# The backward pass of a gated S4 block: h reloaded, parameter sums shared with GpSimd, gradient stores grouped, w2 padded in DRAM

## The chip, the cores and the metric

One core of a Trainium2 chip. The metric is the device time of one launch in microseconds, the median of the runs shown.

## The reference, cut to what matters

The kernel computes the forward pass and all gradients (a vjp) of

```python
xn  = layernorm(x)                                  # x: 2048 x 576
s   = fftconv(xn, K) + xn * Dskip                   # K[d,l] = Re sum_n C[d,n] exp(dtA[d,n] l) dtB[d,n], n = 0..127
h   = silu(xn @ w1) * (xn @ w3)                     # w1, w3: 576 x 4608
out = x + s * silu(h @ w2)                          # w2: 4608 x 576
```

with respect to x, A, B, C (each 576 x 128, real and imaginary), log_dt, Dskip, w1, w3 and w2. Data is bfloat16. out_0 is the output, out_1 the gradient of x, out_2 to out_9 those of the state space parameters, out_10, out_11, out_12 those of w1, w3, w2.

## The kernel before, in words

Rows are positions, in 16 tiles of 128. The forward builds the convolution kernel K, keeps its factors in DRAM (Q_dram, PZ_dram), computes gate and up for all positions and keeps them in DRAM (GI_dram), and h too (H_dram, read by the forward's own w2 product at L774 through DMA transposes named hc). The convolution is done with DFT matrices: spectra of xn (UH_dram) and of K (KH_dram), products of spectra on VectorE (cmul_acc, L594), inverse transforms on TensorE (idft_tile, L573).

The backward (L1066) interleaves four strands of work:

- *The feed-forward loop*, 18 groups of 256 hidden columns. phase6_load (L1125) loads gate and up for a group (gg_n, h_n), makes silu (gu_n) and its derivative on ScalarE in place, and multiplies on VectorE: L1153 makes derivative times up, L1154 makes h again as silu times up, in place. It also loads two row tiles of w2 into one of four padded SBUF rows (L1139, GpSimd's queue) and transposes them by DMA (w2T). phase6_group (L1157) multiplies by w2 (L1172), scales (L1178), and stores the two gradients of the hidden layer (GU_dram, GG_dram). phase6_grad2 (L1188) makes the gradient of w2, phase6_grad13 (L1206) those of w1 and w3; each result is copied from PSUM by ScalarE into a buffer gw or gw2 and stored through GpSimd's queue (L1205, L1222, L1231).
- *The convolution's backward* (conv_bwd_quarter, L866), four quarters of the channels. a3 holds a spectrum in three planes, the third a copy made on VectorE (spectrum_variants, L588). It multiplies the gradient by xn on VectorE (L893) for the gradient of Dskip, forms spectra products, transforms them back, and ScalarE writes each 128 x 144 result into gk_st by four instructions with strided outputs (L926, L927). A second set of products yields the gradient of xn (gx, started at L941, finished at L947, stored at L948).
- *The parameter sums* (param_quarter, L950), 36 chunks of 16 channels. Q is loaded by DMA transpose (qT), TensorE multiplies it with gK (L970) into two PSUM tiles T, VectorE multiplies these with PZ into pr_q (L977, four times per half chunk) and reduces each pr_q of 1024 numbers to 16 (L979, twice per half chunk). phase5_final (L982) comes after all chunks: it turns the sums S_all into the parameter gradients, for five blocks of up to 128 channels, and reloads the parameters for it.
- *The input gradient* (phase6_inputs, L1234), after the loop, 16 tiles: GG and GU come back through DMA transposes (ggc, guc), are multiplied by the transposed w1 and w3 (px, L1262), summed with gx from GXN_dram (L1265) and taken back through the layernorm (ln_bwd_tile, L1270). The transposed weights are in two parts: the first FA = 12 of 36 chunks are loaded early (wTA), the rest when the loop's buffers are free (wTB; the profile shows both under the name wTB_w).

What sets the order: each engine and each DMA queue runs its instructions in order. `self.at(us)` (L83) gives what follows a priority, in us, and the program's instructions are put in order by it as their inputs allow. The last call gives the numbers: backward(560, 36, 90, 15, 18, ...) puts groups 36 apart from 560, quarters of the convolution 90 apart, chunks 15 apart after the four quarters (from 920), and input tiles 18 apart after the loop (from 1208). Buffers come from pools with a number of buffers each; a tile waits until the one `bufs` before it is done. Pools of one side lie one upon the other, so a new pool waits for what lay there before. SyncE's queue (SP) carries all DMA transposes (nat_transpose, L1122) and most loads and stores.

Of the kernel before, what the change touches and what calls it, by code (L numbers as in the profile page):

```python
# [11 lines left out]
ALU = mybir.AluOpType  # L12
# [48 lines left out]
class K:  # L61
# [246 lines left out]
    def compute_W(self, pool, c, dsz):  # L308
        nc, cfg = self.nc, self.cfg
        N = cfg.N  # L310
        v = slice(0, dsz)
        Wr = pool.tile([P, N], FP32, name="Wr_c")
        Wi = pool.tile([P, N], FP32, name="Wi_c")
        t2 = pool.tile([P, N], FP32, name="Wt2")
        dtc = self.dt_col[v, c:c + 1]
        nc.vector.tensor_tensor(out=Wr[v], in0=self.C_re[v, c, :], in1=self.B_re[v, c, :], op=ALU.mult)
        nc.vector.tensor_tensor(out=t2[v], in0=self.C_im[v, c, :], in1=self.B_im[v, c, :], op=ALU.mult)
        nc.vector.tensor_tensor(out=Wr[v], in0=Wr[v], in1=t2[v], op=ALU.subtract)
        nc.vector.tensor_scalar(out=Wr[v], in0=Wr[v], scalar1=dtc, scalar2=None, op0=ALU.mult)
        nc.vector.tensor_tensor(out=Wi[v], in0=self.C_re[v, c, :], in1=self.B_im[v, c, :], op=ALU.mult)  # L320
        nc.vector.tensor_tensor(out=t2[v], in0=self.C_im[v, c, :], in1=self.B_re[v, c, :], op=ALU.mult)
        nc.vector.tensor_tensor(out=Wi[v], in0=Wi[v], in1=t2[v], op=ALU.add)
        nc.vector.tensor_scalar(out=Wi[v], in0=Wi[v], scalar1=dtc, scalar2=None, op0=ALU.mult)
        return Wr, Wi

# [262 lines left out]
    def spectrum_variants(self, A2, Az):  # L588
        nc = self.nc
        nc.vector.tensor_copy(out=A2[:, :, 1], in_=A2[:, :, 0])  # L590
        nc.vector.tensor_copy(out=A2[0:1, :, 1, 0, :], in_=Az[0:1, :, 0, :])
        nc.vector.memset(Az[0:1, :, 0, :], 0.0)

# [85 lines left out]
    def ffn_scratch(self):  # L679
        cfg = self.cfg  # L680
        D, DT, L, LT, FT = cfg.D, cfg.DT, cfg.L, cfg.LT, cfg.FT
        F = cfg.F
        self.FG = 256
        self.GI_dram = self.dram.tile([F // self.FG, P, 2, LT, self.FG], BF16, name="GI_dram")
        self.H_dram = self.dram.tile([LT, P, F], BF16, name="H_dram")
        self.GS_dram = self.dram.tile([4, P, LT, D // 4], BF16, name="GS_dram")
# [44 lines left out]
    def forward_tail(self, T0, TB, TQ, gctx):  # L731
# [19 lines left out]
        with pool(name="g_all", bufs=1, side="right") as gp, pool(name="o_ep", bufs=3, side="right") as ep, \  # L751
# [9 lines left out]
            with pool(name="o_ep1", bufs=1) as ep1, pool(name="o_h", bufs=2) as hp, \  # L761
# [4 lines left out]
                for n, t_ in enumerate(w2g):  # L766
                    nc.gpsimd.dma_start(out=t_[:], in_=aps["B_w2"][n * GRP * P:(n + 1) * GRP * P, :].rearrange(
                        "(c p) d -> p c d", p=P))
                for i0 in range(0, LT, 2):
# [69 lines left out]
    def ssm_bwd_conv(self, T0, TQ, ps):  # L839
# [3 lines left out]
        with self.tc.tile_pool(name="b_k", bufs=1, side="right") as kp, self.tc.tile_pool(name="b_z", bufs=2, side="right") as zp:  # L843
# [7 lines left out]
            for g in range(4):  # L851
                self.conv_bwd_quarter(g, kp, zp, ps, T0 + g * TQ, TQ)

    def ssm_bwd_params(self, T0, TC, S_all, ps):
        cfg = self.cfg
        D, LT = cfg.D, cfg.LT
        with self.tc.tile_pool(name="g_k", bufs=1, side="right") as gkp, self.tc.tile_pool(name="g_q", bufs=2, side="right") as qp:
# [5 lines left out]
            for g in range(4):  # L863
                self.param_quarter(g, gz, S_all, qp, ps, T0 + TC * g * D // 64, TC)

    def conv_bwd_quarter(self, g, kp, zp, ps, T0, TQ):  # L866
# [10 lines left out]
        for b in range(NB):  # L877
            a3 = kp.tile([P, 3, KT, W], BF16, name=f"a3_{b}")
            nc.sync.dma_start(out=a3[:, 1], in_=self.UH_dram[g, b, :, 0])
            nc.sync.dma_start(out=a3[:, 0], in_=self.UH_dram[g, b, :, 1])  # L880
            A2[b], Az[b] = a3[:, None, 1:3], a3[:, None, 0]
            self.spectrum_variants(A2[b], Az[b])
# [6 lines left out]
        for b in range(NB):  # L889
            prod = zp.tile([P, KT, W], BF16, name="gsxn")  # L890
            for tt in range(KT):
                t = b * KT + tt
                nc.vector.tensor_tensor(out=prod[:, tt, :].rearrange("p (h d) -> p h d", h=2),  # L893
# [12 lines left out]
        for i in range(NB - 1, -1, -1):  # L906
            self.at(T0 + TQ * (0.2 + 0.1 * (NB - 1 - i)))
# [12 lines left out]
            for oc in range(KT):  # L920
                t = i * KT + oc
                pt = ps.tile([P, 512], FP32, name="et_ps")
                self.idft_tile(pt, ZZ, oc)
                for h in range(2):
                    pv = pt[:, h * W // 2:(h + 1) * W // 2].rearrange("p (c d) -> p c d", d=8)
                    nc.scalar.activation(out=st[:, :, 0, :, h, t], in_=pv, func=ACT.Copy, scale=1.0 / 512)  # L926
                    nc.scalar.activation(out=st[:, :, 1, :, h, t], in_=pv, func=ACT.Copy, scale=self.lcol[:, t:t + 1])  # L927
# [7 lines left out]
        for j in range(NB):  # L935
            self.at(T0 + TQ * (0.6 + 0.1 * j))
# [3 lines left out]
            gx = zp.tile([P, KT, W], FP32, name="gx")  # L940
            nc.vector.tensor_tensor(out=gx[:], in0=gs[:, j * KT:(j + 1) * KT, :],  # L941
                                    in1=self.dskip_row[:, None, cs].to_broadcast([P, KT, W]), op=ALU.mult)
            for oc in range(KT):
                t = j * KT + oc
                pt = ps.tile([P, 512], FP32, name="et_ps")
                self.idft_tile(pt, Z, oc)
                nc.vector.tensor_tensor(out=gx[:, oc, :], in0=pt[:, 0:W], in1=gx[:, oc, :], op=ALU.add)  # L947
            nc.scalar.dma_start(out=self.GXN_dram[:, j * KT:(j + 1) * KT, cs], in_=gx[:])  # L948

    def param_quarter(self, g, gz, S_all, qp, ps, T0, TC):  # L950
# [3 lines left out]
        for cc in range(NQ):  # L954
# [6 lines left out]
            qT = qp.tile([P, 16, N], BF16, name="qT")  # L961
# [426 lines left out]
```

## Time and profile before

| | |
|---|---|
| median of 2 runs | 2041.88 us (2040.19 to 2043.56) |
| the profiled execution, its own time | 2058.91 us |
| its span, first to last instruction | 2057.1 us |
| mean granted TensorE clock | 0.947 |
| PE busy | 1772.9 us (86%) |
| DVE busy | 1428.3 us (69%) |
| ACT busy | 992.8 us (48%) |
| POOL busy | 366.5 us (18%) |
| DMA moved | 416.06 MB, mean 202 GB/s |

PE is TensorE's matmuls, PEld its weight loads, DVE VectorE, ACT ScalarE, POOL GpSimd, SP SyncE; a q behind the name is the engine's queue or sequencer. In a row of the timeline stand the start, the duration, the engine, the line of the kernel, and what is written from what. In a row of waits stand who waited for whom, and then us in total, times, and the longest. A row of stages has the stretch, its length, each engine's busy time with the number of instructions, the TensorE clock granted, the busy share of the DMA engines (above 1 means several packets in flight on one) and GB/s.

### The profile page before, as it was taken

How to read it: one execution, taken by the hardware profiler on the slowest of the kernel's cores; microseconds unless marked ns; L12 is line 12 of the kernel's file. 1: busy time of each engine (PE TensorE's matmuls, PEld its weight loads, DVE VectorE, ACT ScalarE, POOL GpSimd, SP SyncE). 2: the span in 40 equal slices, each digit the busy share in tenths (PEclk: the TensorE clock that was granted, in tenths of full speed). 3: DMA queues.
4: the chain of work that ended last, by engine and by line, in shares of the span. 5: the costliest groups of instructions: out<-in, count | busy, mean ns of one | idle time of the engine just before them, and what ended most of it. 6: DMA issues, size and time to landing. Idle time of an engine off the chain costs nothing. (4 is left out here: it accounts for less than half of the span.)

```text
span 2057.1 us, 42197 instructions
## 1 busy us (share of the span) xinstructions
PE 1772.9 (86%) x17174; PEld 1300.8 (63%) x17174; DVE 1428.3 (69%) x2772; ACT 992.8 (48%) x1668; POOL 366.5 (18%) x540
## 2 busy tenths in 40 slices
PE   2889999999699995999898998898899939989992
PEld 1534444444488874778777777786678727767771
DVE  7548888888287723686874868676789635858667
ACT  2778888888445544765646556343355200000000
POOL 4003333333312102111111211222111200000000
PEclk9999999999799997999999999999899969999996
DMA  3678888896957568465563655798898599999970
GB/s 83 204 290 301 306 298 302 290 320 248 283 140 175 136 139 260 125 179 168 165 179 96 195 155 164 196 264 205 183 208 203 163 232 216 198 216 226 208 150 22
DMA packets 595505, 416.06 MB, mean 202 GB/s; under 512 B 404912, under 2 KB 537136, under 8 KB 590704
## 3 DMA queue, kind: packets, MB, share of 16 engines
q1 hardware_dynamic: 539632, 264.00, 53.6%
q0 software_dynamic: 30544, 120.94, 17.2%
q10 hardware_dynamic: 25136, 28.44, 5.5%
q8 instruction: 134, 2.20, 0.4%
q14 instruction: 59, 0.48, 0.1%
HBM read 133.01 MB, written 188.01 MB: 156 GB/s over the span
## 5 line engine op out<-in xcount | busy, mean ns | idle before, releaser
L719 PE MATMUL pgu<-wmB_w,xnT 128*128 128x512 bf16 x1152 | 284.1, 382 | 1.1 <-ACT E_k L392 1.1
L1262 PE MATMUL px<-wTB_w,guc 128*128 128x288 bf16 x1152 | 243.7, 292 | 36.4 <-DMA guc<-GU_dram 24.1
L1262 PE MATMUL px<-wTB_w,ggc 128*128 128x288 bf16 x1152 | 245.3, 292 | 15.0 <-DMA wTB_w<-in_B_w_dram 9.1
L1218 PEld LDWEIGHTS <-xn_bf 128*128 128x128 bf16 x2304 | 226.2, 98 | 48.7 <-issue 20.7
L977 DVE TENSOR_TENSOR pr_q<-et_ps,pz 128x512 f32<-128x512 f32 x288 | 186.6, 680 | 96.2 <-PE et_ps L970 96.0
L1172 PE MATMUL ph<-w2T,goT 128*128 128x256 bf16 x1440 | 192.3, 286 | 8.8 <-ACT gh L1175 6.5
L719 PEld LDWEIGHTS <-xnT 128*128 128x128 bf16 x1152 | 103.5, 98 | 125.2 <-issue 20.9
L1279 ACT ACTIVATE t<-gx 128x576 f32<-128x576 f32 x16 | 10.9, 683 | 346.0 <-DVE gx L1265 311.3
L979 DVE TENSOR_REDUCE S_all<-pr_q 128x16 f32<-128x1024 f32 x144 | 173.9, 1211 | 0.4
L1200 PE MATMUL pgw<-go_o,h_n 128*128 128x288 bf16 x1152 | 160.9, 294 | 8.7 <-DVE h_n L1154 8.7
L1172 PEld LDWEIGHTS <-goT 128*128 128x128 bf16 x1440 | 144.1, 103 | 33.8 <-issue 7.8
L1262 PEld LDWEIGHTS <-guc 128*128 128x128 bf16 x1152 | 114.1, 100 | 68.9 <-DMA guc<-GU_dram 26.1
L1221 ACT CAST gw<-pgw 128x256 bf16<-128x256 f32 x144 | 53.7, 378 | 212.5 <-PE pgw L1218 169.7
L784 PE MATMUL po<-w2g,hc 128*128 128x288 bf16 x1152 | 148.9, 286 | 2.6 <-DMA hc<-H_dram 2.6
L1218 PE MATMUL pgw<-gg_n,xn_bf 128*128 128x256 bf16 x1152 | 132.5, 276 | 14.2 <-ACT gw L1221 14.2
L1262 PEld LDWEIGHTS <-ggc 128*128 128x128 bf16 x1152 | 113.8, 100 | 45.4 <-issue 9.6
L1200 PEld LDWEIGHTS <-h_n 128*128 128x128 bf16 x1152 | 113.9, 100 | 39.0 <-DVE h_n L1154 9.2
L1218 PE MATMUL pgw<-gu_n,xn_bf 128*128 128x256 bf16 x1152 | 132.3, 272 | 3.4 <-ACT gw L1221 2.0
L784 PEld LDWEIGHTS <-hc 128*128 128x128 bf16 x1152 | 111.5, 98 | 30.2 <-DMA hc<-H_dram 3.1
L722 ACT ACTIVATE s_t<-pgu 128x512 bf16<-128x512 f32 x144 | 87.4, 609 | 55.2 <-PE pgu L721 54.7
L1222 POOL DMA_DIRECT2D out_dram<-gw x144 | 77.7, 541 | 187.1 <-ACT gw L1221 184.0
L1175 ACT CAST gh<-ph 128x512 bf16<-128x512 f32 x144 | 83.7, 613 | 50.8 <-PE ph L1172 35.9
(305 smaller groups left out, 3726.1 us busy)
## 6 DMA issues: line engine op xcount, KB each, us to landing
GI_dram<-gu_t POOLq DMA_DIRECT2D x72, 512.0 KB, 5.7
H_dram<-h_t SPq DMA_DIRECT2D x72, 256.0 KB, 5.2
Q_dram<-q_k SPq DMA_DIRECT2D x36, 512.0 KB, 5.3
gg_n<-GI_dram POOLq DMA_DIRECT2D x18, 1024.0 KB, 5.7
h_n<-GI_dram POOLq DMA_DIRECT2D x18, 1024.0 KB, 8.7
GU_dram<-gu_n SPq DMA_DIRECT2D x36, 512.0 KB, 4.2
GG_dram<-gg_n SPq DMA_DIRECT2D x36, 512.0 KB, 7.5
E_dram<-E_k SPq DMA_DIRECT2D x18, 768.0 KB, 3.6
```

What stands on the lines that cost most here:

```text
L719: nc.tensor.matmul(pgu[:, j], lhsT=xnT[:, c, ts], rhs=wm[w][:, c, :], start=(c == 0), stop=False)
L722: nc.scalar.activation(out=s_t[:, :, q, :], in_=pgu[:, 0].rearrange("p (g f) -> p g f", g=ng), func=ACT.Silu)
L784: nc.tensor.matmul(pos[k][:, pi_, 0:pw], lhsT=hcs[k][:, fi, :], rhs=w2[fi][:, po:po + pw], start=(fi == 0), stop=(fi == FT - 1))
L977: nc.vector.tensor_tensor(out=pr[:, r], in0=T[r][:], in1=pz[:, s + r, h * 8:h * 8 + 8, :][:, :, None, :] .to_broadcast([P, 8, 2, AV]), op= ...
L979: nc.vector.tensor_reduce(out=S_all[:, 2 * s:2 * s + 2, d0:d0 + 8].rearrange("p k d -> p d k"), in_=pr[:].rearrange("p r d k a -> p d k r ...
L1172: nc.tensor.matmul(ph[j][:, k, :].rearrange("p (a f) -> p a f", f=P), lhsT=lw, rhs=rh, start=(n == 0), stop=(n == nfull))
L1175: nc.scalar.copy(out=gh[:, j], in_=ph[j][:])
L1200: nc.tensor.matmul(pgw[pi_][:, 0:pw], lhsT=hn[:, tt, fl * P:(fl + 1) * P], rhs=go_o[:, tt, po:po + pw], start=(tt == 0), stop=(tt == LT - 1))
L1218: nc.tensor.matmul(pw_[:, 0:FG], lhsT=self.xn_bf[:, tt, c * P:(c + 1) * P], rhs=nat[:, tt, :], start=(tt == 0), stop=(tt == LT - 1))
L1221: nc.scalar.copy(out=gw[:], in_=pw_[:, 0:FG])
L1222: nc.gpsimd.dma_start(out=aps[oname][c * P:(c + 1) * P, fb:fb + FG], in_=gw[:])
L1262: nc.tensor.matmul(px[pi_][:, 0:pw], lhsT=act[:, fi, :], rhs=wT[part][ai][:, f, po:po + pw], start=(fi == 0 and ai == 0), stop=(fi == FT - ...
```

## The change

- w2 is written to DRAM in the forward, padded from 576 to 640 columns (W2P_dram), from the tiles that the forward's w2 product uses; the backward transposes it from there. The four padded rows in SBUF go.
- L1154 goes. After L1153 h is loaded again from H_dram into the buffer of up.
- Convolution backward: the third plane of a3 is loaded, the corrections of one row go to GpSimd, and so do the products at L893 and the start of gx. Two inverse transforms share a PSUM bank; ScalarE copies them densely into a new buffer and GpSimd spreads them into gk_st. gx is stored in the natural order of the channels by two DMAs on SyncE's queue. New priorities spread the products evenly.
- Parameter sums: in each half chunk the first pr_q is folded by an addition on GpSimd, and VectorE reduces 512 numbers instead of 1024. qT has three buffers, pr_q a pool of its own; pz is loaded by SyncE's queue instead of ScalarE's. The final stage becomes final_block, called per block as soon as its chunks are there; its DMAs are on GpSimd's queue.
- Gradient stores go to ScalarE's queue; the four column tiles of w1's and w3's gradients are stored by one DMA.
- FA becomes 9. The priorities of the backward become backward(560, 40, 96, 15, 18, ...). In the input gradient the sum is made in place.

```diff
@@ forward_tail
+                wz = ep1.tile([P, 1, DT * P - D], BF16, name="wz")
+                nc.gpsimd.memset(wz[:], 0.0)
+                w2p = self.W2P_dram.rearrange("(c p) d -> p c d", p=P)
+                self.at(T0 + 150)
+                nc.sync.dma_start(out=w2p[:, :, D:DT * P], in_=wz[:].to_broadcast([P, FT, DT * P - D]))
+                for n, t_ in enumerate(w2g):
+                    nc.sync.dma_start(out=w2p[:, n * GRP:(n + 1) * GRP, 0:D], in_=t_[:])
@@ conv_bwd_quarter
-            nc.sync.dma_start(out=a3[:, 1], in_=self.UH_dram[g, b, :, 0])
-            nc.sync.dma_start(out=a3[:, 0], in_=self.UH_dram[g, b, :, 1])
+            for j, r in ((0, 1), (1, 0), (2, 0)):
+                nc.sync.dma_start(out=a3[:, j], in_=self.UH_dram[g, b, :, r])
...
-            self.spectrum_variants(A2[b], Az[b])
+            nc.gpsimd.tensor_copy(out=a3[0:1, 2, 0, :], in_=a3[0:1, 0, 0, :])
+            nc.gpsimd.memset(a3[0:1, 0, 0, :], 0.0)
...
-                nc.vector.tensor_tensor(out=prod[:, tt, :].rearrange("p (h d) -> p h d", h=2),
+                nc.gpsimd.tensor_tensor(out=prod[:, tt, :].rearrange("p (h d) -> p h d", h=2),
...
-            for oc in range(KT):
-                t = i * KT + oc
+            self.at(t0 + TQ * (0.0425 * (NB - i) + 0.06))
+            sd = sp.tile([P, KT, 2, W], BF16, name="gk_sd")
+            for o2 in range(0, KT, 2):
+                t = i * KT + o2
                 pt = ps.tile([P, 512], FP32, name="et_ps")
-                self.idft_tile(pt, ZZ, oc)
+                for j in range(2):
+                    self.idft_tile(pt[:, j * W:(j + 1) * W], ZZ, o2 + j)
+                nc.scalar.activation(out=sd[:, o2:o2 + 2, 0, :], in_=pt[:, 0:2 * W].rearrange("p (t d) -> p t d", t=2),
+                                     func=ACT.Copy, scale=1.0 / 512)
+                for j in range(2):
+                    nc.scalar.activation(out=sd[:, o2 + j, 1, :], in_=pt[:, j * W:(j + 1) * W], func=ACT.Copy,
+                                         scale=self.lcol[:, t + j:t + j + 1])
+            for k in range(2):
                 for h in range(2):
-                    pv = pt[:, h * W // 2:(h + 1) * W // 2].rearrange("p (c d) -> p c d", d=8)
-                    nc.scalar.activation(out=st[:, :, 0, :, h, t], in_=pv, func=ACT.Copy, scale=1.0 / 512)
-                    nc.scalar.activation(out=st[:, :, 1, :, h, t], in_=pv, func=ACT.Copy, scale=self.lcol[:, t:t + 1])
+                    nc.gpsimd.tensor_copy(out=st[:, :, k, :, h, i * KT:(i + 1) * KT],
+                                          in_=sd[:, :, k, h * W // 2:(h + 1) * W // 2].rearrange(
+                                              "p t (c d) -> p c d t", d=8))
@@ param_quarter
+                prs = []
                 for s in range(2):
-                    pr = qp.tile([P, 2, 8, 2, AV], FP32, name="pr_q")
+                    pr = rp.tile([P, 2, 8, 2, AV], FP32, name="pr_q")
...
-                    nc.vector.tensor_reduce(out=S_all[:, 2 * s:2 * s + 2, d0:d0 + 8].rearrange("p k d -> p d k"),
-                                            in_=pr[:].rearrange("p r d k a -> p d k r a"), op=ALU.add, axis=AX.XY)
+                    prs.append(pr)
+                nc.gpsimd.tensor_tensor(out=prs[0][:, 0], in0=prs[0][:, 0], in1=prs[0][:, 1], op=ALU.add)
+                out = lambda s: S_all[:, 2 * s:2 * s + 2, d0:d0 + 8].rearrange("p k d -> p d k")
+                nc.vector.tensor_reduce(out=out(1), in_=prs[1][:].rearrange("p r d k a -> p d k r a"), op=ALU.add, axis=AX.XY)
+                nc.vector.tensor_reduce(out=out(0), in_=prs[0][:, 0], op=ALU.add, axis=AX.X)
+            self.at(T0 + TC * (cc + 2))
+            ready(ch)
@@ backward
-        FA = 12
+        FA = 9
...
-            gwp = ffn.enter_context(pool(name="e_gw", bufs=4))
-            rowp = ffn.enter_context(pool(name="e_w2r", bufs=1))
+            gwp = ffn.enter_context(pool(name="e_gw", bufs=2))
...
-            self.ssm_bwd_params(T1, TC, S_all, ps)
-            self.at(T1 + TC * D // 16)
-            self.phase5_final(out, fix, S_all, ps)
+            self.ssm_bwd_params(T1, TC, fix, S_all, ps)
@@ phase6_load
-            w2r = self.w2rows[fi % len(self.w2rows)]
-            nc.gpsimd.dma_start(out=w2r[:, 0:D], in_=aps["B_w2"][fi * P:(fi + 1) * P, :])
-            self.nat_transpose(w2T[:, fl], w2r[:])
+            self.nat_transpose(w2T[:, fl], self.W2P_dram[fi * P:(fi + 1) * P, :])
...
-            nc.vector.tensor_tensor(out=hn[:, sl, :], in0=gu[:, sl, :], in1=hn[:, sl, :], op=ALU.mult)
+        nc.gpsimd.dma_start(out=hn[:], in_=self.H_dram[:, :, gi * FG:(gi + 1) * FG].rearrange("t p f -> p t f"))
@@ phase6_grad13
+            gw = gwp.tile([P, nfull, FG], BF16, name="gw13")
...
-                gw = gwp.tile([P, FG], BF16, name="gw13")
-                nc.scalar.copy(out=gw[:], in_=pw_[:, 0:FG])
-                nc.gpsimd.dma_start(out=aps[oname][c * P:(c + 1) * P, fb:fb + FG], in_=gw[:])
+                nc.scalar.copy(out=gw[:, c, :], in_=pw_[:, 0:FG])
+            nc.scalar.dma_start(out=aps[oname][0:nfull * P, fb:fb + FG].rearrange("(c p) f -> p c f", p=P), in_=gw[:])
```

## The prediction

> **What bounds the kernel now.** I read the page first: TensorE is busy 86% of a span of 2057.1 us, no other engine over 69%. So TensorE's work, 1773 us, is a floor that the change leaves (it removes no matmul), and only the 284 us in which TensorE stands idle can be won. The next view says where: busy time of each engine by stage. The boundaries are the first backward group, the first sum chunk of the parameter gradients, the last dense-gradient matmul, the end of the gap after it, and the last input-gradient matmul.
>
> ```profile
> core 0: us, PE busy (x) PEld busy (x) DVE busy (x) ACT busy (x) POOL busy (x), PEclk, DMA share, GB/s
> 560.00:795.00 235.00, 215.05 (x2173) 179.52 (x2172) 149.44 (x301) 110.53 (x192) 41.73 (x87) 0.96 0.62 154
> 795.00:1317.00 522.00, 464.54 (x4658) 395.67 (x4656) 370.70 (x769) 315.89 (x714) 92.11 (x170) 0.95 0.56 168
> 1317.00:1641.30 324.30, 291.66 (x3005) 245.38 (x3004) 238.32 (x336) 141.06 (x235) 66.54 (x117) 0.96 0.89 205
> 1641.30:1712.00 70.70, 27.46 (x242) 19.65 (x241) 28.25 (x40) 1.15 (x3) 1.07 (x2) 0.71 1.11 225
> 1712.00:2017.50 305.50, 290.05 (x2666) 229.83 (x2666) 212.58 (x412) 13.20 (x32) 0.00 (x0) 0.97 1.07 195
> 2017.50:2057.10 39.60, 0.22 (x2) 0.00 (x0) 26.66 (x141) 1.35 (x3) 0.00 (x0) 0.56 0.09 20
> ```
>
> Length minus PE busy gives TensorE's idle time: 20, 57, 33, 43, 15 and 39 us; the other 76 lie before 560 us, in code that the diff leaves alone. Third, the waits of TensorE (and one of ScalarE) in the two loop stages: us in total, times, longest.
>
> ```profile
> PE et_ps L582 <- ACT gk_st L927: 20.7, 22, 3.2
> PE et_ps L582 <- DVE gx L947: 9.8, 4, 3.6
> PE pgw L1200 <- DVE h_n L1154: 8.7, 1, 8.7
> ...
> PE et_ps L970 <- DMA qT<-Q_dram: 14.7, 4, 8.9
> PE pgw L1218 <- ACT gw L1221: 10.6, 3, 5.0
> ...
> ACT gw L1221 <- DMA out_dram<-gw: 23.4, 6, 7.1
> ```
>
> The first three are of the convolution stage: TensorE waits for PSUM banks that ScalarE empties in thin strided slices. The others are of the parameter stage: late transposes, and a staging buffer whose store has not landed. Fourth, the gap, in SyncE's timeline, and the tail, in VectorE's (start, us).
>
> ```profile
> 1659.32 33.77 SPq L1123 DMA_TRANSPOSE wTB_w<-in_B_w_dram  x10
> ...
> 2039.58 0.44 DVE L1265 TENSOR_TENSOR gx<-px,gxs 128x288 f32<-128x288 f32 x1
> 2039.94 0.27 DVE L1045 TENSOR_TENSOR ft<-ST,C_re_bf 64x128 f32<-64x128 f32 x1
> 2040.14 0.27 DVE L1048 TENSOR_SCALAR gout<-gr,dt_col 64x128 bf16<-64x128 f32 x1
> 2043.55 0.82 DVE L1291 SCALAR_TENSOR_TENSOR o<-t,rstd,go 128x576 bf16<-128x576 f32 x1
> ```
>
> TensorE is done at 2017.5, but the last tile's layernorm begins at 2039.6: it stands in VectorE's queue behind the small instructions of the final parameter block. That block, not the input gradient, sets the end.
>
> **What the Trainium skill says.** "SBUF — State Buffer", Who interferes with whom: a VectorE instruction with two SBUF inputs and a GpSimd instruction that reads SBUF lock each other out whole. The trace fits and doesn't prove it: the small GpSimd copy of L642 takes 346 ns in the median, 1130 at most. "GPSIMD Engine Reference", 3.1 Elementwise: two-input work costs about 2.6 cycles an element, about twice VectorE; the trace agrees (L247, 640 f32: 1.53 us). "TensorE: Matmul & The Clock Gate", Part 1: idle windows halve TensorE's clock; the trace agrees, with PEclk 0.71 in the gap against 0.95 to 0.97 in the dense stages. So an idle us saved brings somewhat more than itself. "DMA: Bandwidth & Descriptors", Issuing engines are not separate DMA queues: moving stores from GpSimd's queue to ScalarE's saves issue time, not bandwidth; nothing here shows it alone.
>
> **The change part by part**, against the profiled execution (2058.9 us, of which 1.8 lie outside the span).
>
> *Tail.* phase5_final is split into blocks that start when their chunks are summed. By the priorities, the last chunk moves from 36 us ahead of the last input tile to about 69 (chunks end at 944+36x15=1484, tiles at 1280+18x16=1568; before 1460 and 1496), and only two blocks are left by then: about 2 x 48 instructions x 0.25 us = 24 us of VectorE, in a stage where it is free 30% of the time. The last layernorm then runs from 2017.6 to 2022.4 (its own 4.8 us) and its store lands 5.2 us later (median of that issue): tail 10.5 instead of 39.6 us, **-29**. If the 12.7 us from the last store's issue to the end belong to that store, -21.
>
> *Convolution stage (522 us).* ScalarE's 256 strided copies (gk_st, 84 us of union) become 32 of 288 and 64 of 144 elements, about 32x0.40+64x0.25=29 us; GpSimd does the strided scatter, 64 copies of 288 elements. The trace has no such copy: by its 0.35 us for 144 elements on one partition 0.6 us, by the two-input rate 0.9; I take 0.8, 51 us. Nothing waits for it but the gK stores, a quarter ahead of their readers. Two transforms share a bank, so banks are freed sooner: the 20.7 goes, and half of the 9.8. VectorE loses the variant copies (9), gsxn (10), gx's start (12) and L1154 (72 x 0.66=48 over the loop): about 61 of its 371 us in this stage. On GpSimd the products cost 64x0.4=26 and gx's starts 16x1.6=26 us; if every GpSimd read locks VectorE out, its load returns to some 420 of 522, still under TensorE's 465. The extra a3 load (16 x 144 KB) is hidden by a DMA share of 0.56. Sum: -20.7-5-4 (gh copies behind the strided ones)-6 (gw waits)=**-36**.
>
> *h reloaded.* Not a product any more: a 1 MB load in 512 B pieces on GpSimd's queue, after L1153. I estimate 12 us to landing (512 KB stores with the same pieces: 4.2 and 7.5 us), less about 2 us of products that fall away. In before, L1154 ends 6 to 33 us ahead of the group's first L1200 (6.1, 10.8, 11.4 in the tightest), so ten us later costs some 4 us in one group and the first group's start: **+8**. Both ends: 0, if VectorE's relief brings L1153 forward; +46, if the load takes 20 us (the sum of what each group then lacks).
>
> *Parameter stage (324 us).* Per chunk VectorE did 8 x 0.65 + 4 x 1.21 = 10.0 us; two of the four reductions halve to about 0.65: 8.9. GpSimd's addition of 512 f32 is about 1.26 us by L247, and has two products and a full reduction (2.5 us) to hide behind; later than that by over 1.1 us, VectorE stalls one for one, and after three banks TensorE (L970). The PSUM tiles are freed 1.2 us earlier. Kernel gradients are staged by four, with one store instead of four, on ScalarE's queue: the waits for landed stores (23.4 and the 10.6 behind it) go; ScalarE gets 6 issues a group at about 0.4 us, hidden since it is busy 141 of 324. A third qT buffer and pz off ScalarE take half of the 14.7. About 22.4 chunks run before the input tiles instead of 17.8: 4.6 x 1.4 us of TensorE comes in. Less cold clock in both loop stages: -8 (estimate, from PEclk 0.95). Sum: -10.6-7+6.4-8=**-19**. The spread of the h loads over a DMA share of 0.89 is in the +8 and its upper end.
>
> *Gap.* FA 12 to 9 makes wTB 27 chunks instead of 24: 33.8 x 27/24, +4.2. By the pools' sizes the ggc tiles then lie over e_in only, not over the gw buffers, so the first transpose need not wait for the store that landed at 1648.6: up to -7, or -3 behind the qT already queued. **0**, from -10 to +8.
>
> *Input gradient.* 1.6 chunks fewer, in-place sum, pz no longer blocking ScalarE's loads: **-4** of the 15 us idle and the chunks' own time; final blocks in VectorE's 93 free us could cost as much.
>
> *Forward.* w2 padded: 10 writes on SyncE's queue past the hc transposes, 4608 pieces of 128 B among them, about 10 us of transfers under a DMA share of 0.62; hc loads now cost TensorE 2.6 us: **+4**, 0 to 10. GpSimd loses 36 w2r loads and their 122 us of waits. Memsets, pools and smaller buffers elsewhere: nothing on the chain.
>
> Sum: -29-36+8-19+0-4+4 = -76; I take **-73**, since a chain relieved shows the next wait. 2058.9-73=1986 for a profiled execution. The median of the runs shown, 2041.88, is 17.0 below the profiled one; the same difference gives **1969 us**.
>
> **Rivals.**
> - *Only the tail is won* (0.2). The h load takes 20 us in a DMA share near 0.9: loop stages -36-19+46=-9, with -29-4+4: -38, 2004; if GpSimd's new copies also cost TensorE 15 through locked-out VectorE, -23: 2019. For: 0.89 and 1.07 DMA share from 1317 us on. Against: eight groups had over 18 us to spare.
> - *The loop closes up* (0.12). with VectorE and ScalarE spread out TensorE reaches 97% here (from 300 to 350 us of the forward it is busy 49.67 of 50): of the loop's 90 idle us 65 go, 15 of cold clock, 11 in the gap, with the tail's 29: -120, 1922. Against: each relieved wait has another close behind.
> - *Slower* (0.08): GpSimd's queue holds up the loop. The h load waits in it for L1153, behind the eight activations (group 3: 911.1 to 922.7, 11.6 us); scatters, additions and products queued behind wait too, VectorE's reductions for them, and TensorE for banks. Two thirds of 11.6 us in 18 groups is 139: 2042-73+139=2108. It is slower than now from 4.1 us of lost TensorE per group, by 2% from 6.3. Against: GpSimd is busy 67 of 324 us, and additions can be queued ahead of the load.
>
> **How the numbers follow.** The forecast has 0.6; its own range is 1940 to 2000. The whole range, 1925 to 2025, leaves out the slower rival (0.08), part of the first rival (0.06) and part of the second (0.05). About 2% is what a measurement can tell from no change: under 2001 lie nearly all of the forecast (0.57), the second rival (0.12) and part of the first (0.06): 0.75; slower 0.07; within 2% 0.18.
>
> **What would show it.** Tail about 10 us, with the last layernorm right behind the last px. In the convolution stage no TensorE wait for gk_st, and PE busy near 93%. L1200 waiting for a DMA of h in one or two groups, not ten. TENSOR_REDUCE of half size near 0.65 us, not starting late behind GpSimd. A wTB row of about 38 us. I am wrong if h_n's DMA or a GpSimd addition leads the waits of TensorE or VectorE, or if the tail is still set by a parameter block.

## The result and the profile after

Measured: 2176.24 us (2171.02 and 2181.46) against 2041.88, a ratio of 1.0658 (95% interval 1.0542 to 1.0774): slower, where 1969 was forecast. The profiled execution took 2171.02 us, its span is 2169.2. (Medians and ratios of the runs further down leave out executions more than 1.5% above the fastest of the same kernel.) Busy time by stage of the changed kernel, with the boundaries of before (first backward group, first sum chunk, last dense-gradient matmul, end of the gap, last input-gradient matmul):

```profile
core 0: us, PE busy (x) PEld busy (x) DVE busy (x) ACT busy (x) POOL busy (x), PEclk, DMA share, GB/s
802.00:1380.00 578.00, 482.70 (x4737) 408.50 (x4736) 361.02 (x578) 277.47 (x570) 209.10 (x218) 0.91 0.61 174
1380.00:1730.50 350.50, 296.83 (x3026) 246.06 (x3027) 231.41 (x382) 131.66 (x224) 75.95 (x78) 0.92 0.93 216
1730.50:1796.50 66.00, 27.39 (x257) 19.98 (x256) 25.75 (x37) 0.37 (x1) 7.59 (x6) 0.66 1.07 219
1796.50:2162.10 365.60, 293.79 (x2573) 229.33 (x2569) 199.24 (x460) 13.65 (x34) 59.46 (x72) 0.91 1.00 159
2162.10:2169.20 7.10, 0.04 (x1) 0.00 (x0) 3.86 (x8) 0.78 (x2) 0.00 (x0) 0.87 0.06 21
```

The spans of the two profiled executions differ by 112.1 us, less than the medians' 134, because the profiled execution of before was 17 us above its median and that of the changed kernel 5 below. With each stage's exact ends in both traces the 112.1 us are: forward +7.9, convolution stage +43.0, parameter stage +38.3, gap +0.6, input gradient +54.6, tail -32.3. TensorE runs the same 17174 matmuls; their busy time grew by 24 us, at a granted clock of 0.91 and 0.92 instead of 0.95 to 0.97 in the three long stages, in which it now stands idle for 95, 54 and 72 us. What it waits for in the loop (us, times, longest):

```profile
PE ph L1176 <- ACT gh L1179: 41.5, 12, 14.0
PE pgw L1223 <- DVE gu_n L1182: 19.5, 6, 12.1
PE pgw L1204 <- DMA h_n<-H_dram: 13.2, 2, 9.2
PE pgw L1223 <- ACT gw L1225: 12.2, 3, 7.8
PE et_ps L564 <- DVE ZZ L922: 11.7, 4, 7.1
PE ph L1176 <- DMA w2T<-W2P_dram: 11.3, 1, 11.3
PE et_ps L900 <- POOL gsxn L896: 11.2, 24, 0.7
```

The waits for gk_st, 20.7 us before, are gone, as forecast; several others stand in their place. The list ranks waits, not losses: the wait for gh, 6.5 us before, stays at 37 to 49 us in three versions below (f2, g2, g4) whose loops are about as short as before the change. In the input-gradient stage VectorE waits for the staging buffers of the final blocks, and here is one such wait in its timeline (start, duration, idle time before and its releaser in brackets), with what SyncE had in flight:

```profile
1953.68 0.29 DVE L1049 TENSOR_SCALAR gout<-gri,dt_col 128x128 bf16<-128x128 f32 x1 [13.48 <-DMA out_dram<-gout]
```

```profile
1937.74 22.56 SPq L1129 DMA_TRANSPOSE guc<-GU_dram  x1
```

VectorE waits 13 us for a 32 KB store in the middle of a layernorm; TensorE's gap at 1946.1 is 19.4 us long. What else was in flight then is taken up with the runs e4 and e9. The gap's transposes on SyncE and the tail are what was forecast, the last layernorm right behind the last px:

```profile
1744.59 37.93 SPq L1129 DMA_TRANSPOSE wTB_w<-in_B_w_dram  x10
```

```profile
2162.06 0.82 DVE L1268 TENSOR_TENSOR gxs<-px,gxs 128x288 f32<-128x288 f32 x2 [2.69 <-PE px L1265]
2165.39 0.82 DVE L1292 SCALAR_TENSOR_TENSOR o<-t,rstd,go 128x576 bf16<-128x576 f32 x1
```

### The profile page after: what moved, and what is told of

Its sections match the earlier page's. It is cut to its first block, busy times and chain, and to the rows that moved or that the text cites. A ratio compares the mean times of both kernels' runs of the same rounds, so it can differ in the third digit from the quotient of the medians.

```text
span 2169.2 us, 41932 instructions
## 1 busy us (share of the span) xinstructions
PE 1797.2 (83%) x17174; PEld 1311.5 (60%) x17174; DVE 1373.1 (63%) x2538; ACT 941.3 (43%) x1508; POOL 554.3 (26%) x616
## 5 line engine op out<-in xcount | busy, mean ns | idle before, releaser
L1223 PEld LDWEIGHTS <-xn_bf 128*128 128x128 bf16 x2304 | 231.0, 100 | 75.8 <-issue 40.3
L1265 PE MATMUL px<-wTB_w,ggc 128*128 128x288 bf16 x1152 | 248.3, 296 | 31.7 <-DVE gxs L1268 13.4
L1265 PE MATMUL px<-wTB_w,guc 128*128 128x288 bf16 x1152 | 247.4, 296 | 23.8 <-DMA wTB_w<-in_B_w_dram 12.8
L1204 PE MATMUL pgw<-go_o,h_n 128*128 128x288 bf16 x1152 | 165.5, 299 | 22.1 <-DMA h_n<-H_dram 13.2
L999 POOL TENSOR_TENSOR pr_q<-pr_q 128x512 f32<-128x512 f32 x72 | 93.1, 1292 | 354.1 <-DVE pr_q L996 254.9
L1281 ACT ACTIVATE t<-gxs 128x576 f32<-128x576 f32 x16 | 10.9, 684 | 388.7 <-DVE gxs L1268 388.7
L1223 PE MATMUL pgw<-gu_n,xn_bf 128*128 128x256 bf16 x1152 | 140.2, 281 | 25.9 <-DVE gu_n L1182 19.5
L1265 PEld LDWEIGHTS <-ggc 128*128 128x128 bf16 x1152 | 115.4, 101 | 63.5 <-issue 21.4
L1265 PEld LDWEIGHTS <-guc 128*128 128x128 bf16 x1152 | 115.3, 101 | 56.9 <-issue 13.2
L705 POOL DMA_DIRECT2D GI_dram<-gu_t x72 | 68.5, 952 | 211.3 <-DVE gu_t L701 109.1
L988 PE MATMUL et_ps<-gz,qT 128*128 128x64 bf16 x1152 | 53.9, 198 | 68.4 <-DVE pr_q L996 52.1
```

The costliest lines, as they stand in the source:

```text
L705: nc.gpsimd.dma_start(out=self.GI_dram[fb * ng:(fb + 1) * ng, :, :, i0:i0 + NT, :].rearrange("g p u t f -> p u g (t f)"), in_=gu_t[:].rear ...
L988: nc.tensor.matmul(T[r][:, dd].rearrange("p k (f t) -> p (k f) t", f=2), lhsT=qT[:, dl, :], rhs=gK[:, r, :, :, dl, :].rearrange("p k f t - ...
L999: nc.gpsimd.tensor_tensor(out=prs[0][:, 0], in0=prs[0][:, 0], in1=prs[0][:, 1], op=ALU.add)
L1204: nc.tensor.matmul(pgw[pi_][:, 0:pw], lhsT=hn[:, tt, fl * P:(fl + 1) * P], rhs=go_o[:, tt, po:po + pw], start=(tt == 0), stop=(tt == LT - 1))
L1223: nc.tensor.matmul(pw_[:, 0:FG], lhsT=self.xn_bf[:, tt, c * P:(c + 1) * P], rhs=nat[:, tt, :], start=(tt == 0), stop=(tt == LT - 1))
L1265: nc.tensor.matmul(px[pi_][:, 0:pw], lhsT=act[:, fi, :], rhs=wT[part][ai][:, f, po:po + pw], start=(fi == 0 and ai == 0), stop=(fi == FT - ...
```

## The experiments

The first theory was written from these traces: gout's staging costs the input gradient its 55 us, GpSimd's and ScalarE's queues cost the loop its 81. Its rivals were the additions on GpSimd, VectorE slowed by GpSimd, and the planned order. Each run is named by a label (e1, f1, g1 and so on). Times are medians, ratios (with 95% intervals) are to the kernel before, run beside them. Stage lengths are of one profiled execution each, which lies between 16 us above its run's median (e10) and 10 below it (e13). Executions of one of these kernels lie up to 28 us apart (2149.72 to 2177.63), so 10 us of a single run are not read. An edit can also shift the order that the planner writes. In the cuts of code, - is the changed kernel, + the run, and ... marks what is left out.

**The final blocks' transfers.**

```
-tile_pool(name="gfo", bufs=2   +tile_pool(name="gfo", bufs=8
```

> The changed kernel with eight staging buffers instead of two for the outputs of the final parameter blocks (gout, gl); their stores stay on GpSimd's queue. Theory (VectorE waits for a buffer whose store has not landed, 66 us in five waits, and TensorE for VectorE): the input-gradient stage falls from 365.6 to 305 to 320 us, one gap of 12 us in the loop goes too, in all 45 to 65 us off 2176, no wait for gout left over 3 us. Rival (it is the additions on GpSimd, or the chunks that now lie in this stage, which cost TensorE its time): the waits move to pr_q or et_ps and the time falls by less than 15 us.

2273.17 us (1.1113, 1.1058 to 1.1169), 97 slower. No wait for gout is left, but with the larger pool 12 chunks now run in a row (1816 to 1951), and px waits for them and 48.6 us more. That the larger pool lies over memory of px's tiles is the likely reason, and not shown. So the run does not test the theory. In a row half a chunk costs 4.4 to 5.0 us, more where a block runs between.

```
-nc.gpsimd.dma_start(out=aps["out_8"][do...   +nc.sync.dma_start(...     # e4
-nc.gpsimd.dma_start(out=aps[oname][do...     +nc.scalar.dma_start(...   # e9, and out_8
```

> The changed kernel with one store moved: gl (128 pieces of two bytes) goes on SyncE's queue instead of GpSimd's. Buffers stay at two; order on every other engine is unchanged. Theory (the two-byte pieces, which take 20 us to land, stand ahead of the gout stores in the same queue): gout lands in about 2 us in the median instead of 6 to 7, the long waits go, 40 to 60 us off. Rival (gout lands late on GpSimd's queue by itself, or for DMA load): gout still lands up to 20 us late, 0 to 15 us off. Third: the buffer that is waited for is gl's own or the wait moves to SyncE's transposes behind the store: slower or the same.

> The changed kernel with the gout and gl stores on ScalarE's queue, two buffers as they are; TensorE's and SyncE's order unchanged. Theory one (stores of 256 B pieces land late on GpSimd's queue while the transposes of SyncE keep the DMA engines busy, and land in 2 us on ScalarE's): gout waits gone, stage 310 to 325 us, 40 to 55 us off. Theory two (the DMA engines are busy with the transposes, whatever queue a store is on): it lands up to 20 us late here too, and the stage stays at 350 or more; as the move also lets ScalarE wait, it may be slower.

2178.64 (1.0654, 1.0583 to 1.0725) and 2169.55 (1.0619, 1.0545 to 1.0693): nothing. It is not the queue: gout still takes up to 19.4 us to land when gl stands in another queue, and up to 16.9 on ScalarE's. That agrees with what the Trainium skill says in "DMA: Bandwidth & Descriptors", Issuing engines are not separate DMA queues: DMAs of all queues run on the same DMA engines.

Both runs move the store of two-byte pieces (gl), and neither takes it away. The traces point at it. This one is issued 2 us ahead of the long guc transpose above and lands 20.2 us later; below it are the core's stretches from 1940 on:

```profile
1935.97 0.54 POOL L1070 DMA_DIRECT2D out_dram<-gl  x1 [0.17 <-issue]
1940.00:1945.00 5.00, 5.00 (x43) 3.99 (x41) 0.20 (x2) 0.14 (x2) 0.10 (x1) 1.00 2.45 32
1945.00:1950.00 5.00, 1.07 (x9) 0.61 (x7) 0.00 (x0) 0.00 (x0) 0.00 (x0) 0.89 1.89 2
1950.00:1956.00 6.00, 0.00 (x0) 0.00 (x0) 2.04 (x7) 0.00 (x0) 1.72 (x4) 0.50 1.22 17
```

While gl is in flight the DMA engines count as busy (share 2.45 to 1.22) and move 32, 2 and 17 GB/s; the stage's mean is 159. All five such stores of the changed kernel (us):

| gl issued at | lands after | long transpose issued behind it | TensorE's gap |
|---|---|---|---|
| 1660.5 | 18.1 | none in flight | 12.1, at 1670.3 |
| 1936.0 | 20.2 | guc, 22.6 | 19.4, at 1946.1 |
| 2019.4 | 19.9 | guc, 20.7 | 17.0, at 2028.1 |
| 2105.1 | 22.6 | ggc, 18.6 | 13.4, at 2128.4 |
| 2143.8 | 10.3 | none in flight | none |

These are TensorE's only gaps of over 12 us from 1380 us on, outside the gap stage, and the only transposes of over 9 us from 1330 on. All ten gout stores seen to take over 10 us were issued between 0.7 us ahead of a gl store and 5.1 behind it; those seen in flight without one landed within 8.5. In all traces of changed versions, 71 of 71 gout stores that took over 12 us were issued at most 2 us ahead of a gl store or 12 behind it. The rival is that the transposes make both kinds of store late. Against it stand the first and the last row, where gout took 16 to 17 and 10 to 12 us, and the tail of the kernel before: without transposes, gout took 1.4 to 2.3 us, but the one behind the two-byte stores there (gl_bf, issued at 2039.7 and 2040.1) took 14.1:

```profile
2041.21 0.47 ACTq L81 DMA_DIRECT2D out_dram<-gout  x1
DMA to landing us min/median/max: 1.4/1.5/14.1
```

The second line is of all gout stores of before. So the late landings go with the two-byte store, which the change issues five times in busy stages instead of once at the end. That it is the cause was not tested: no version leaves it out or puts it at the end.

```
-bufs=2 (gfo)  +bufs=5;  -junk = new("junk")  +junk = t1;  -g = new("gri")  +g = grho     # e7
as e7, gfo bufs=6, and  -X = fp.tile(...  +X = xp.tile(...  (bufs=2);  qT bufs 3 -> 2     # e13
```

> The changed kernel with five gout buffers instead of two, in the same memory (junk shares ft1, gri shares grho), so that the chunks stay spread over the input tiles. Theory (VectorE waits for gout stores, TensorE for VectorE): no gout wait over 3 us, the input-gradient stage 305 to 325 instead of 365.6 us, about 2115 to 2135 in all. Rival (VectorE's own work per chunk and block, about 11 us a chunk when the chunks came in a row, is what TensorE waits for): 350 us or more.

> The changed kernel with six gout buffers, two buffers of the rates (so that a block's loads go out a block ahead) and, to make room, two qT buffers instead of three. Theory (the final blocks' transfers land late behind SyncE's transposes, whatever queue they are on, and VectorE waits for them in order; with five gout buffers alone the wait moved to the rates, 27 us): no wait of VectorE over 5 us for gout or rates, the input-gradient stage 310 to 330 us instead of 366. Rival (the stage is bound by the transposes of ggc and guc themselves, which share the DMA engines with the chunks' qT): TensorE's waits move to guc, stage 345 or more.

e7: 2167.77 (1.06, 1.0536 to 1.0665), stage 354.4. The wait only moved on:

```profile
DVE Wr_c L1030 <- DMA rates_c<-in_A_C_re_dram: 26.8, 2, 26.6
```

e13, with the rates' loads a block ahead: 2136.26 (1.0469, 1.0402 to 1.0535), stage 335.8: 30 of its 55 us. What VectorE still waits for there:

```profile
DVE S_all L1002 <- POOL pr_q L999: 28.1, 16, 12.8
```

So more buffers and earlier loads win back about half of the stage's loss (the edit also takes a qT buffer away, and this profile is 10 us below its run's median). The wait for the addition that comes next is not the addition's own time, which is 1.27 us. It stands in GpSimd's queue behind the blocks' loads, and these stand still for 12.6 us, shortly after a gl store issued at 1981.45. The longest wait, 12.8 us, ends with

```profile
2000.50 0.53 POOL L1014 DMA_DIRECT2D rates_c<-in_A_B_im_dram  x1 [12.58 <-issue]
2001.56 1.27 POOL L999 TENSOR_TENSOR pr_q<-pr_q 128x512 f32<-128x512 f32 x1
```

**GpSimd's queue and GpSimd's work.**

```
-nc.gpsimd.tensor_copy(out=a3[0:1, 2... / memset   +nc.vector. ...        # e2
-nc.gpsimd.dma_start(out=hn[:], in_=self.H_dram...  +hn = gu * hn, DVE    # e3
```

> The changed kernel with the one-row corrections of the u spectra (a copy and a memset on one partition, four blocks a quarter) on VectorE instead of GpSimd. Theory (the correction waits in GpSimd's queue for a late spectrum load, 59 us in seven waits, and the loads of gg_n, h_n and h stand behind it, so ScalarE and then TensorE wait): 15 to 35 us off the convolution stage (578), no idle stretch of over 6 us at the quarters' changes. Rival (what TensorE lacks there is VectorE's pace, slowed by GpSimd's copies): unchanged within 8 us, or slower, since VectorE now waits for the same load itself.

> The changed kernel with h formed on VectorE again (silu times the second factor) and not reloaded; nothing else edited, but the planned order shifts with it. Theory (the reload is a small part of the loss: 9 us at the first group, 4 at the eighth, and some of the late loads behind it on GpSimd's queue): 10 to 25 us off in the loop stages. Rival one (the reload is what holds up the loop): 60 us or more off. Rival two (the reload is a gain, VectorE's 48 us come back on the path): 10 us or more slower.

e2: 2164.43 (1.0584, 1.0515 to 1.0654), the loop unchanged (932.9 against 928.6): the row correction in GpSimd's queue was not a cause, though 58.8 us of that queue's waits stood behind it. e3: 2139.14 (1.0459, 1.0409 to 1.0509). The first group's last dense-gradient matmul ends at 862 instead of 879 (850 before). The middle groups end only 6 to 12 us sooner, the convolution stage is 8 us shorter, and the loop 17.

```
-nc.gpsimd. ...   +nc.vector. ...        # gsxn, gx's start, a3's corrections
-scalar.activation(out=sd ...), 4 gpsimd copies   +scalar.activation(out=st[:, :, 0, :, h, t + j], in_=pv ...) from PSUM
```

> The changed kernel with the convolution stage's work taken off GpSimd altogether: gsxn, gx's start and the row corrections on VectorE, the strided gk_st written by ScalarE straight from PSUM (256 slices, as before the change; two transforms still share a bank). Theory (GpSimd's copies and products lock VectorE out: its products took 1.22 instead of 0.75 us next to them, and TensorE waits 12 us for ZZ and 11 us for gsxn): the stage (q0 minus the first group, 578 us) falls to 545 to 560, ZZ and gsxn waits below 8 us together, VectorE's products back to 0.75 us. Rival (the stage lost its time to the h reload, the later forward and the changed order, not to GpSimd): 570 or more, and ScalarE's gk_st waits of 20 us come back.

2139.68 (1.0506, 1.044 to 1.0572). The stage falls by 24 us to 554.7, as the theory had it, and VectorE's products are back; TensorE's waits for ZZ and gsxn are below 1 us. As h is still reloaded here, the reload is not what slowed the products. Groups by shape in the convolution stage, first of the changed kernel, then of this one (busy us, mean ns, idle before):

```profile
L583 DVE TENSOR_TENSOR cm_t<-g,a 128x1152 bf16<-128x1152 bf16 x80 | 64.1, 814 | 0.0
```

```profile
L583 DVE TENSOR_TENSOR cm_t<-g,a 128x1152 bf16<-128x1152 bf16 x80 | 59.3, 756 | 0.0
```

The eight groups of two-input products (six of the spectra, two of L1182) take 284.0 us before, 320.6 after, 286.7 here. But at 1400 to 1430 ScalarE then waits 21.4 us until a transfer of wT has landed, TensorE 15.2 for ScalarE, and at the loop's end 5 of the 24 us are left in the profiled execution. That one was the slowest of four, 2155.72 us; by its median the run is 37 us faster than the changed kernel.

```
-nc.gpsimd.tensor_tensor(out=prs[0][:, 0], ... op=ALU.add); half reduction   +full reduction on VectorE
```

> The changed kernel with the addition of the two products on GpSimd (L999) undone: both reductions of a half chunk are full ones on VectorE. Theory (the addition stands between VectorE's products and its second reduction, and VectorE waits for it; the chain that ended last goes product, addition, reduction, product, 4.5 us a half chunk in the loop's second part): 10 to 25 us off the parameter stage (350) and the input-gradient stage (366) together. Rival (the half reductions are worth their wait; before the change a half chunk took VectorE 5.0 us): 5 to 20 us slower.

2161.31 (1.0598, 1.0532 to 1.0664): parameter stage 12 longer, input gradient 22 shorter, 10 together; alone hardly to be told from nothing. The 22 are not VectorE's waits for the addition, which come to 3.1 us in that stage of the changed kernel and to 10.0 in the parameter stage. Where the addition is on the path, the changed kernel's chain of waits shows it (start, us):

```profile
1425.43 1.30 DVE pr_q L996 x2
1426.80 1.27 POOL pr_q L999
1428.10 0.69 DVE S_all L1002
```

Here the planned order puts the half reduction (L1002) directly behind the products, and the full one (L1001), which was to hide the addition, elsewhere.

**The gradient stores.**

```
-nc.scalar.dma_start(out=aps["out_12"]... (and L1226, L1235, L1236)   +nc.gpsimd (e5) / nc.sync (e6)
```

> The changed kernel with the stores of the dense kernel gradients (L1209, L1226, L1235, L1236) issued from GpSimd's queue again, as before the change; staging by four stays. Theory ([...]a late transfer of SyncE holds up ScalarE, and TensorE's banks with it: gh 41.5 us, gw 26 us of TensorE's waits in the loop): those two waits fall below 25 us together and the loop from 928.6 to 870 to 895 us. Rival (ScalarE is late for its silu, whose load waits on GpSimd's queue): gh stays at 30 to 45 us and the loop within 10 us, or grows, as more stands on GpSimd's queue.

> The changed kernel with the same gradient stores issued from SyncE's queue. Theory (ScalarE held up by its own stores): gh and gw waits fall as on GpSimd's queue and the loop loses 30 to 55 us, unless SyncE, which now waits for the gradients itself, is late with w2T, qT or the spectra: then these lead TensorE's waits instead. Rival (silu's late load): gh stays, loop within 10 us.

2192.86 (1.0723, 1.0657 to 1.0788) and 2165.1 (1.0606, 1.0531 to 1.0681); the waits for gh stay at 42.8 and 38.9 us. The theory falls.

**Do they add up, and the plan.** f1 joins the edits of e3, e10, e13 and e5; f2 adds the plan's numbers of before, f3 has those alone:

```
-backward(560, 40, 96, ...)  +backward(560, 36, 90, ...)
-t0 = T0 + TQ * (0.15 + 0.0425 * (...)[...]); second self.at   +T0 + TQ * (0.2 + 0.1 * ...), (0.6 + 0.1 * j)
```

> The changed kernel with four parts undone or mended together: h formed again on VectorE, the convolution stage's work off GpSimd, six gout and two rates buffers (qT two), gradient stores on GpSimd's queue. The plan's numbers stay as changed. Theory (the losses are separate and add up; alone they were worth 17 us in the first group, 24 us in the convolution stage, 30 us in the input-gradient stage, and the stores on ScalarE's queue show only where the other load on GpSimd's queue is gone, 10 to 20): 2080 to 2105 us. Rival (each relieved wait is taken up by the next one, as the stage gains vanished by the loop's end in the single runs): 2120 or more.

> The same four parts, and the plan's numbers as before the change too (36 and 90 instead of 40 and 96, and the convolution's due times of before). Theory (what is left of the loss in the loop, some 30 us, lies in the planned order: groups of 64 to 71 us next to groups of 45): the loop comes to 850 to 870 us, 2030 to 2060 in all, and with the tail at 7 us about even with the kernel before or better. Rival (the plan's numbers do not matter): within 10 us of the run with four parts alone.

> The changed kernel with the plan's numbers of before alone (36 and 90, due times of the convolution). Theory (the planned order costs some 30 us of the loop): 2135 to 2155. Rival one (the numbers do not matter): within 10 us of 2170. Rival two (the new numbers were made for the new work, and the old ones bring the loads later still): 2185 or more.

f1: 2110.92 (1.0343, 1.0275 to 1.0412), loop 889.7: between the two bounds. It is 65 us faster than the changed kernel, where the four runs alone come to 97 (e3 37, e10 37, e13 40, e5 17 slower), so about two thirds add. f2: 2081.18 (1.0178, 1.0128 to 1.0228). The loop, 855.2, is back near 847, as forecast; the whole is 21 us above the forecast. Its two parts:

```profile
799.00:1337.00 538.00, 469.57 (x4751) 399.95 (x4750) 370.83 (x734) 328.03 (x730) 61.75 (x100) 0.95 0.58 168
1337.00:1654.00 317.00, 284.36 (x2911) 238.03 (x2910) 215.88 (x325) 131.18 (x224) 80.59 (x96) 0.96 0.84 197
```

f3: 2155.18 (1.0542, 1.0488 to 1.0595), 21 us faster. In its profile the old numbers take 25 us from the loop (17.0 instead of 20.3 chunks lie in it) and 26 from the input gradient, and give 16 back in the gap, where the first final block now falls, and 29 in the tail, where a block is last again.

**The rest.** All three are f2 with one or two more edits: the stores on ScalarE's queue again (g2), FA 12 (g1), FA 12 and no addition on GpSimd (g4).

> The version with four parts and the plan's numbers of before, but with the gradient stores on ScalarE's queue as in the change; TensorE's order is the same. Against that version (loop 855 us): theory one (a store on ScalarE waits for a DMA semaphore shared with SyncE's transfers and holds up gh and gw copies behind it): loop 10 to 25 us longer, TensorE's waits for gw back above 15 us. Theory two (it makes no difference once the other parts are mended): within 6 us. Theory three (GpSimd's queue, with 36 more waits in it, delays the loads of gg_n): 6 us or more shorter, and gh (43.7) falls.

> The version with four parts and the plan's numbers of before, with FA 12 again instead of 9, so that 24 instead of 27 chunks are transposed in the gap. Theory (the gap of 87.5 us is as long as its transposes, some 3.8 us each ten chunks' block aside): gap 76 to 84. Rival (the gap is long since guc's first transpose took 19 us beside the chunks' loads): 85 or more.

> The same with FA 12 and with the addition on GpSimd undone too: what is left of the change is the blocks spread, two transforms a bank, the stores staged by four, w2 padded in the forward and the in-place sum. Theory (a half chunk's wait for the addition, 30 us of VectorE's waits in the input-gradient stage with one TensorE gap of 14 us, goes; before the change the same reductions fitted): 2045 to 2070. Rival (VectorE, 0.5 us a half chunk slower, is now late itself): 2075 or more. It beats the kernel before only if the gap also shrinks to 70.

g2: 2070.37 (1.0118, 1.0067 to 1.0169), loop 836.8 against 855.2: ScalarE's queue costs nothing and is, if anything, the better place. g1: 2071.13 (1.017, 1.0102 to 1.0238), gap 79.6. g4: 2057.03 (1.0071, 1.0047 to 1.0094), 14 below g1; by the profiles 11 us of it lie in the input gradient. In g1 VectorE waits there 32.1 us for the addition; 28.6 of it are two waits in which the addition stands behind GpSimd's loads, as in e13. g4's loop is 843, its input gradient 317.8, its tail 19.9, but its gap 79.0 instead of 65.4, because the 24 chunks took 48.01 us where before they took 33.77. The first of the ten transposes makes the difference, issued 5 us behind a gl store; the other nine take 31 together:

```profile
1651.34 0.54 POOL L1064 DMA_DIRECT2D out_dram<-gl  x1 [4.48 <-DVE gout L1043]
1656.58 17.17 SPq L1123 DMA_TRANSPOSE wTB_w<-in_B_w_dram  x1
```

f2, f3 and g1 have one such transpose in the gap too (18.5 to 19.0 us), the kernel before and the change have none.

**One part on the kernel before.** The spread blocks alone (the changed kernel's final_block and its calls, eight gout buffers, FA 9):

> The kernel before, with one part of the change alone: final parameter blocks spread over the input-gradient stage (phase5_final replaced by the blocks of the changed kernel, eight gout buffers, stores and rates' loads on GpSimd's queue), and, to make room, FA 9 instead of 12. No h reload, no new work on GpSimd in the loop. Theory (the tail's 32 us are won by this part, and it loses its time only where VectorE waits for its transfers): loop unchanged at 847, gap +4, tail 7 to 10 instead of 39 us, input-gradient stage 311 to 335: 2010 to 2035 in all, the first version faster than the kernel before. Rival (blocks in this stage always cost what the tail gives): stage 345 or more, 2045 or more in all.

2212.67 (1.0843, 1.0781 to 1.0904). The loop takes 856 us (847 before), the tail 6.9; but as in e1, 15 chunks run in a row (1753 to 1904), and px goes on only after them. It does not tell whether the blocks alone would gain. No version tried beat the kernel before.

## Why the prediction was wrong, step by step

- *Tail, -29*: right; -32.3, for the reason given.
- *Gap, 0*: right; +0.6, the wTB row 37.93 us, 38 forecast, and it starts 3.9 us sooner after the loop.
- *Forward, +4 (0 to 10)*: in the range; +7.9, and it shows as TensorE's wait of 11.3 us for the first w2T (2.2 before).
- *Input gradient, -4*: the step that failed most, +54.6 (measured at 365.6 us, against 311.0). It priced the blocks by VectorE's busy time ("93 free us") and gave no time to the landing of their stores, for which there are two buffers. VectorE waits 73.6 us for gout in this stage, with px's sum queued behind, and TensorE's three long gaps there come to 49.8. e13 wins 30 of the 55 with more buffers and earlier loads. Each of the three gaps follows a two-byte store of a final block; the prediction says nothing of these stores, and that they make the others late is seen in the traces and not tested.
- *h reloaded, +8*: the mechanism was right, the first group's term too small: 17 us there and 17 in the loop (e3). TensorE waited twice for a load of h, 13.2 us. The upper end, ten late groups, did not come.
- *Convolution stage, -36*: failed, +43.0, of which 8 are h's (e3). The gk_st wait did go. "still under TensorE's 465" was the error: VectorE need not be the busiest engine to be late, when each product of a chain is slower and TensorE waits for its end (ZZ 11.7, gsxn 11.2). The scatter was mis-sized as well: 64 copies at 1.50 us in the mean, 93.3, not 0.8 and 51. e10 gives 24 us of the stage to GpSimd's work; with both undone (f1) it is 36 shorter.
- *Parameter stage, -19*: failed, +38.3, for reasons known in part. The addition has not the full reduction to hide behind, since the order is the planner's; VectorE waits 10.0 us for it. The first two-byte store falls here, at 1660.5, with a TensorE gap of 12.1. The chunks that come into the loop (20.3, not 22.4) were priced at TensorE's 1.4 us; with the plan's old numbers alone (f3) the stage, with 3.3 fewer of them and with the first final block behind the loop, is 26 us shorter. That the stores on ScalarE cost nothing was right (g2).
- *Rival "slower: GpSimd's queue holds up the loop"* (0.08, 2108): the right sign; the changed kernel is slower still than it said. The load behind L1153 cost 17 us, not 139, and in the convolution stage the work on GpSimd cost VectorE its pace. Additions queued behind loads, with VectorE's reductions waiting for them, did come, but in the input gradient of e13 and g1, and not in the loop.

The loop's loss is accounted for as a sum (f2, g2, g4), not in single shares: e10's 24 us had shrunk to 5 at the loop's end, e3's 17 fell to 6 and were 17 again, and together with e13 and e5 they made 39 (f1); the plan's numbers made the next 34 (f2). Which wait takes up a single gain was not settled for each. What no run undoes, such as the halved pools e_gw (4 buffers to 2) and l_sm (4 to 2), costs at most what is left in g4, 0.7%.

## What to carry to other kernels

Price a staging buffer by the landing time in the stage where it will be used, and not by a quiet stage's. When a store lands late, list everything in flight each time before the largest transfer is blamed: here the smallest store was the one that was always there, and moving it to another queue did not test it. Work moved to a less busy engine is free only if it neither slows nor precedes a short chain that the bound engine waits for; precedes also means standing in that engine's queue behind DMA issues. Test parts together as well as alone: here the single repairs that helped gave 21 to 40 us each, f1 two thirds of the sum of its parts, and all that was undone together 119.

## What the runs showed of the hardware

GpSimd's strided bf16 copies of 288 elements took 1.19 us in the median and 1.50 in the mean. In the convolution stage, with 154 us of copies and products on GpSimd, VectorE's bf16 products of 1152 elements slowed from 0.75 us to 0.81 to 0.87 in the mean; with that work away (e10) they were at 0.76. That agrees in its direction with what the Trainium skill states in "SBUF — State Buffer", Who interferes with whom, and gives a size: 37 us more on 284. That each pair locks the other out for its whole length is not shown here. A store of 128 two-byte pieces took 10 to 23 us to land on GpSimd's queue, and 13.2 and 19.9 where it was seen on SyncE's and ScalarE's; beside one, the core's DMA engines moved as little as 2 GB/s for 5 us, and gout stores of 128 pieces of 256 bytes took 10 to 23 us, where those seen in flight without one took 1.7 to 8.5.
